# k and q over 128 partitions, transposed in two 64-row tiles; x in eight array tiles; batch 0's convolution on TensorE; PSUM and order changed

## The chip, the cores and the metric

The kernel runs on one core of one Trainium2 chip. The metric is the device time of one execution in microseconds (us). Before the change the median of three runs is 317.77 us (317.33 to 321.48).

The engines of the core run side by side, each with its own queue in order: TensorE (PE in the profile, with its weight loads as PEld), VectorE (DVE), ScalarE (ACT), GpSimd (POOL) and SyncE (SP), which here only issues DMAs. TensorE's results stand in PSUM, from where VectorE and ScalarE take them.

## The reference, cut to what matters

```python
# q, k, v: (8 batches, 8 heads, 576, 64); p: (8, 8, 32, 64); x: (8, 576, 512)
def sm_attn(qq, kk, vv):                       # softmax attention, scale 1/8
    s = scale * qq @ kk.T
    a = exp(s - max(s)); a = a / (sum(a) + 1e-9)
    return a @ vv
packed = sm_attn(p, k, v)                      # 32 rows for each head
attn   = sm_attn(q, packed, packed)            # 576 rows for each head
x      = attn with the heads side by side      # (8, 576, 512)
gate   = sigmoid(sum over kk < 5 of conv_w[kk] * x shifted down by 4 - kk rows)
out    = (gate * (x @ w_val)) @ w_out          # fp32
```

`w_val`, `conv_w` and `w_out` arrive as 64-bit floats and are turned into fp32 (or into a high and a low part) on the chip.

## The kernel before, in words

The eight heads of a batch are two groups `g` of four. In a group the four heads stand on 32 partitions each, so that scores of four heads make one tile of 128 partitions; the 576 rows of a head lie on two halves of 288 columns. A pair tile of PSUM is two banks (`big`, line 165), a single is one bank (`one`, line 168). `PSB` (line 42) sets how many of each there are: two pairs, three singles `mid`, one single `out`, eight banks in all.

The work of a batch is cut into streams, generators that yield after each step (the table `streams`, line 600). Each has a letter:

- `K`, `V`, `Q`, `P`: the loads of k, v, q and p (lines 185 to 204), all issued by SP in the written order. k and q are loaded for each group as 96 partitions x 4 heads x 3 x 128 values; a run of 128 values is two neighbouring rows of a head. For q such a run of 512 bytes stands alone in memory, for k three follow each other.
- `L`: the weights' loads (line 217); `W`, `C`, `O`: their conversion (`value_weights`, `conv_weights`, `out_weights`). `O` adds the two parts of `w_out` with two matmuls by the identity (`summed`, line 258) into a `mid` single, takes the high part off with ScalarE and the low one with VectorE.
- `k`: p is transposed (`turned`, line 324), then k (`transposed`, line 302). A k step is four transposes of 96 rows into one `mid` single, 96 columns each, then one ScalarE copy of 128x384 into `kT`. Six such steps serve a batch. `q` does the same for q.
- `a`: the packed attention (`attn_pack`, line 340): `s` matmuls in eight array tiles of 64 rows x 32 columns (`scores`, line 315) into a pair, maximum on VectorE, exponential on ScalarE, three transposes `at` of the weights by group through a `mid` single, then `pv` through a `mid` single.
- `p`, `s`, `t`: the packed result is transposed, the second attention's scores `s` are made, turned by VectorE in 32x32 blocks, normalised by VectorE, GpSimd and ScalarE, and split into a high and a low part (`attn_out`, `weighted`).
- `w`: `wp`, the packed result times `w_val` by head, into a pair (`packed_values`, line 442).
- `x` (`mixed`, line 457): attention output for the gate, by group and half: four matmuls in four array tiles of 32 rows x 64 columns, into a pair, and a ScalarE copy of 128x576 into `xp`. A batch has four such calls.
- `g` (`gate`, line 489): the convolution of the gate by channel chunk: the first tap on ScalarE, four more on VectorE (one operation of 128x576 each), tanh on ScalarE.
- `v` (`value`, line 509): twelve `val` matmuls of 288 columns into a pair, then gate times value on VectorE, the high part on ScalarE, the low part on VectorE.
- `o` (`project`, line 562): `o`, twelve matmuls of 512 columns for 128 rows of output, a copy of `osb`, a store. For the last batch the accumulators of five chunks are kept open at once in three `mid` singles, the `out` single and half a pair.

The string `ORDER` (line 46) sets the order of everything: a token such as `k3.2` runs two steps of stream `k` for batch 3. `InOrder` (line 82) ties each engine's instructions to this order, SP's DMAs too. Each tile's number of buffers is in `NB` (line 19). In the order before, TensorE's work opens with p's and k's transposes of batch 0, and SP issues two transfers of `w_val`, k's first group, six more transfers of `w_val` and then p.

A float32 matmul shows as two instructions in the trace, a transpose or a matmul on float32r as one.

Of the kernel before, what the change touches and what calls it, by code (L numbers as in the profile page):

```python
# [649 lines left out]
```

## Time and profile before

| | us |
|---|---|
| runs, median of three | 317.77 (317.33, 317.77, 321.48) |
| span of the profiled execution, first to last instruction | 320.0 |
| PE busy | 289.8 (91%) |
| DVE busy | 260.4 (81%) |
| ACT busy | 209.6 (66%) |
| POOL busy | 50.6 (16%) |

The result says no time of its own for the profiled execution beside its span. Busy time is the union of an engine's instructions; PE's ends are modelled and its matmuls overlap, so a busy PE is not PE at its peak. A row of a timeline or of the chain gives start, length, engine, operation, output tile <- input tiles and count. A row of groups gives output <- inputs, partitions x elements, the count, then busy time, mean ns of one, and the idle time of the engine ahead of them with what ended it. All lines of the kernel's own operations stand as L90, the helper `InOrder`, so groups are told by their tiles. TensorE's granted clock is 0.998 of full over the span.

### The profile page before, as it was taken

How to read it: one execution, taken by the hardware profiler on the slowest of the kernel's cores; microseconds unless marked ns; L12 is line 12 of the kernel's file. 1: busy time of each engine (PE TensorE's matmuls, PEld its weight loads, DVE VectorE, ACT ScalarE, POOL GpSimd, SP SyncE). 2: the span in 40 equal slices, each digit the busy share in tenths (PEclk: the TensorE clock that was granted, in tenths of full speed). 3: DMA queues.
4: the chain of work that ended last, by engine and by line, in shares of the span. 5: the costliest groups of instructions: out<-in, count | busy, mean ns of one | idle time of the engine just before them, and what ended most of it. 6: DMA issues, size and time to landing. Idle time of an engine off the chain costs nothing.

```text
span 320.0 us, 7365 instructions
## 1 busy us (share of the span) xinstructions
PE 289.8 (91%) x3012; PEld 211.5 (66%) x3012; DVE 260.4 (81%) x404; ACT 209.6 (66%) x424; POOL 50.6 (16%) x59
## 2 busy tenths in 40 slices
PE   0099977998989999999999999999999999999992
PEld 0067434656748876777876867877677788767881
DVE  0773599989998999899989988996899978868761
ACT  2155267988885678677967794887578755556431
POOL 1330122002300041221002312310023000230000
PEclk9999999999999999999999999999999999999999
DMA  7999999599992176941980697262402012111005
GB/s 170 218 223 268 272 231 226 111 229 172 212 221 87 37 175 136 233 126 66 215 191 35 168 209 170 62 160 81 130 33 68 35 33 69 66 66 35 33 2 165
DMA packets 42476, 43.50 MB, mean 136 GB/s; under 512 B 6085, under 2 KB 36805, under 8 KB 42442
## 3 DMA queue, kind: packets, MB, share of 16 engines
q1 hardware_dynamic: 42442, 43.02, 57.3%
q8 instruction: 24, 0.39, 0.6%
q14 instruction: 10, 0.08, 0.1%
HBM read 33.57 MB, written 9.44 MB: 134 GB/s over the span
## 4 chain that ended last, share of the span: by engine, by line
PE 84%; ACT 5%; DVE 4%; DMA 4%; issue 1%; POOL 1%; SPq 0%; ACTq 0%
PE o L90 32%; PE val L90 15%; PE s L90 6%; PE kpt L90 6%; PE qpt L90 5%; PE x L90 5%; PE pv L90 4%; PE at L90 4%; DMA p<-in_p_dram 2%; PE wp L90 2%; PE wo_sum L90 2%; DMA km<-in_k_dram 2%; ACT sig L90 1%; PE ppTt L90 1%; PE pTt L90 1%; DVE wo_words L90 1%
## 5 line engine op out<-in xcount | busy, mean ns | idle before, releaser
L90 DVE SCALAR_TENSOR_TENSOR sig<-xp,cw,sig 128x576 f32<-128x576 f32 x128 | 108.3, 846 | 7.9 <-ACT sig L90 6.7
L90 PE MATMUL o<-woh,gvh 128*128 128x512 f32 x144 | 58.8, 408 | 0.1
L90 PE MATMUL o<-woh,gvl 128*128 128x512 f32 x144 | 56.5, 393 | 0.0
L90 PE MATMUL o<-wol,gvh 128*128 128x512 f32 x144 | 56.4, 391 | 0.0
L90 PE MATMUL val<-a2h,wph 128*128 128x288 f32 x128 | 39.7, 310 | 0.0
L90 PE MATMUL val<-a2h,wpl 128*128 128x288 f32 x128 | 37.9, 296 | 0.0
L90 PE MATMUL val<-a2l,wph 128*128 128x288 f32 x128 | 37.7, 295 | 0.0
L90 POOL TENSOR_TENSOR t<-t,mx 128x576 f32<-128x576 f32 x16 | 22.5, 1404 | 90.6 <-DVE mx L90 89.1
L90 ACT COPY osb<-o 128x512 f32<-128x512 f32 x34 | 19.8, 581 | 24.3 <-PE o L90 19.3
L90 ACT ACTIVATE sig<-sig 128x576 f32<-128x576 f32 x32 | 22.0, 686 | 20.1 <-DVE sig L90 20.0
L90 PEld LDWEIGHTS o<-woh,gvh 128*128 128x128 f32 x144 | 27.0, 188 | 9.0 <-issue 2.2
L90 DVE SCALAR_TENSOR_TENSOR sig<-sig,val 128x576 f32<-128x576 f32 x32 | 23.8, 743 | 11.2 <-ACT sig L90 6.4
L90 PEld LDWEIGHTS o<-woh,gvl 128*128 128x128 f32 x144 | 27.1, 188 | 6.9 <-DVE gvl L90 0.8
L90 PEld LDWEIGHTS o<-wol,gvh 128*128 128x128 f32 x144 | 27.1, 188 | 4.5
L90 ACT CAST gvh<-sig 128x576 fp32r<-128x576 f32 x32 | 21.6, 676 | 11.3 <-DVE sig L90 10.4
L90 POOL TENSOR_TENSOR t<-t,rs 128x576 f32<-128x576 f32 x16 | 20.6, 1288 | 50.1 <-DVE rs L90 42.8
L90 DVE TENSOR_TENSOR gvl<-sig,gvh 128x576 fp32r<-128x576 f32 x32 | 25.3, 792 | 1.6 <-ACT gvh L90 1.4
L90 PE MATMUL qpt<-ident,qm 96*128 96x96 f32 x192 | 25.7, 259 | 0.9 <-DVE sm L90 0.9
L90 PEld LDWEIGHTS qpt<-ident,qm 96*128 96x128 f32 x192 | 19.6, 146 | 9.9 <-issue 5.0
L90 PE MATMUL kpt<-ident,km 96*128 96x96 f32 x192 | 25.9, 267 | 0.0
L90 PEld LDWEIGHTS val<-a2h,wph 128*128 128x128 f32 x128 | 24.1, 189 | 2.5 <-issue 1.8
L90 PEld LDWEIGHTS kpt<-ident,km 96*128 96x128 f32 x192 | 20.1, 151 | 8.3 <-issue 4.2
(78 smaller groups left out, 509.8 us busy)
## 6 DMA issues: line engine op xcount, KB each, us to landing
km<-in_k_dram SPq DMA_DIRECT2D x16, 576.0 KB, 7.3
vm<-in_v_dram SPq DMA_DIRECT2D x16, 576.0 KB, 8.3
qm<-in_q_dram SPq DMA_DIRECT2D x16, 576.0 KB, 7.4
out_dram<-osb SPq DMA_DIRECT2D x24, 256.0 KB, 2.0
wv_words<-in_moe_w_val_dram SPq DMA_DIRECT2D x8, 256.0 KB, 8.0
wo_words<-in_moe_w_out_dram SPq DMA_DIRECT2D x4, 512.0 KB, 11.6
out_dram<-osb SPq DMA_DIRECT2D x8, 192.0 KB, 3.0
p<-in_p_dram SPq DMA_DIRECT2D x16, 64.0 KB, 8.3
```

Source lines behind the costliest of these rows:

```text
L90: made = getattr(self.engine, op)(*args, **kw)
```

## The change

It alters the layout of k and q, TensorE's tiles, PSUM, where some operations run, and the order:

- k and q are loaded as 128 partitions x 9 x 128 values: partition (head, i) holds 18 neighbouring rows, one run of 4,608 bytes. v stays as it was.
- A k or q step has six transposes of 64 rows, 64 columns each, alternating between the upper and the lower half of the array's rows; the two halves write to the two banks of a pair. The ScalarE copy still has 128x384 elements, reads elements 64 apart, and writes them where `kT` or `qT` wants them (runs of 96 for k, of 3 for q).
- PSUM has three pairs, one `mid` single and one `out` single. Transposes of k and q move from `mid` to pairs.
- `x` takes both groups in one call of a half: eight array tiles of 32 rows x 64 columns, two pairs, two copies. A batch has two calls in place of four. The channels lie in another order for it, and so `w_val`, `conv_w` and `w_out` are loaded or written in that order; `w_out` by two DMAs for each chunk.
- Batch 0's convolution runs on TensorE: the packed result times each tap (GpSimd, into `kx`) is the weight of 8 matmuls for each of five taps and each half, accumulated in PSUM; tanh on ScalarE reads them from there. `gate` does nothing for batch 0. The taps are spread over partitions by 40 small matmuls and a ScalarE copy (`cwb`).
- `out_weights` drops the two matmuls by the identity: the high part comes from the top part, and GpSimd adds the rest.
- The last batch's accumulators lie in one pair, both singles, and half of another pair.
- `ORDER` is new throughout. It begins `L0 P0 K0 k0 W0 k0.2 Q0 k0.2 K0 k0 P1 k0.2 L0 W0.2 ...`: SP issues two transfers of `w_val`, p, k's first group, q's first group.

```diff
-PSB = {'big': 2, 'mid': 3, 'out': 1}
+PSB = {'big': 3, 'mid': 1, 'out': 1}
...
-            m = st[nm, b, g] = tile_of(f"{nm}m", [TP, 4, NA, 2 * D], F32, f"{nm}m_{b}_{g}")
-            sp.dma_start(m, src[b, 4 * g : 4 * g + 4].rearrange(order, a=NA, c=2))
+            m = st[nm, b, g] = tile_of(f"{nm}m", [P, NB9, 2 * D], F32, f"{nm}m_{b}_{g}")
+            sp.dma_start(
+                m, src[b, 4 * g : 4 * g + 4].rearrange("h (i n c) d -> (h i) n (c d)", n=NB9, c=2)
+            )
...
-            yield from from_double(f"wo{c}", words, P)
-            ps, hi = summed(f"wo{c}", words), woh[:, c, :]
-            yield
-            act.mul(hi, ps, 0.5)
+            yield from from_double(f"wo{c}", words, P, 0.5)
+            top, rest = st["top", f"wo{c}"], words[:, :, 0].bitcast(F32)
+            hi, lo = woh[:, c, :], wol[:, c, :]
+            act.mul(hi, top, 0.5)
             yield
             dve.scalar_tensor_tensor(
-                wol[:, c, :], ps, 0.5, hi.bitcast(F32), op0=ALU.mult, op1=ALU.subtract
-            )
+                top, top, 0.5, hi.bitcast(F32), op0=ALU.mult, op1=ALU.subtract
+            )
+            yield
+            pool.tensor_tensor(lo, top, rest, op=ALU.add)
             yield
...
-            for a in range(NA):
-                pt = one(f"{nm}pt_{b}_{g}_{a}")[:, : 4 * TP].rearrange("x (j i) -> x j i", j=4)
-                for j in range(4):
-                    pe.transpose(pt[:, j], m[:, j, a], ident[:TP, :TP])
-                yield
-                act.copy(xT[:, :, TP * a : TP * a + TP], pt)
+            if nm == "k":
+                to = xT.rearrange("x (u j) (a i b) -> x u j i b a", u=2, a=NA, i=32)
+            else:
+                to = xT.rearrange("x (u j) (i a b) -> x u j i b a", u=2, a=NA, i=32)
+            for part in range(NA):
+                pt = big(f"{nm}pt_{b}_{g}_{part}")[:, :, : 64 * NA]
+                for n in range(NA):
+                    for u in range(2):
+                        rows = slice(64 * u, 64 * u + 64)
+                        pe.transpose(
+                            pt[:, u, 64 * n : 64 * n + 64],
+                            m[rows, part * NA + n if nm == "q" else n * NA + part, :],
+                            ident[rows, rows],
+                        )
+                yield
+                act.copy(to[:, :, :, :, :, part], pt.rearrange("x u (n j i) -> x u j i n", n=NA, j=2))
                 yield
...
+            two = [big(f"x_{b}_{half}_{n}") for n in range(2)]
+            for g in range(G):
                 for hl in range(4):
                     pe.matmul(
-                        xps[D * (hl % 2) : D * (hl % 2) + D, hl // 2, :HS],
+                        two[hl // 2][D * g : D * g + D, hl % 2, :HS],
                         pp[heads[hl], g, 0, :],
                         a2[heads[hl], g, hc],
                         start=True,
                         stop=True,
                     )
-                yield
-                act.copy(xp[:, :, half, PAD:], xps[:, :, :HS])
-                yield
+            yield
+            for n in range(2):
+                act.copy(xps[n][:, :, half, PAD:], two[n][:, :, :HS])
+                yield
+
+    def convolved(b):
...
+        for half in range(2):
+            a2 = st["a2", b]
+            two = [big(f"x_{b}_{half}_{n}") for n in range(2)]
+            for back in range(NT):
+                src = (half + back) % 2
+                skip = (back + src - half) // 2
+                for g in range(G):
+                    for hl in range(4):
+                        pe.matmul(
+                            two[hl // 2][D * g : D * g + D, hl % 2, skip:HS],
+                            kx[heads[hl], g, NT - 1 - back, :],
+                            a2[heads[hl], g, src * HS : src * HS + HS - skip],
+                            start=(back == 0),
+                            stop=(back == NT - 1),
+                        )
+            yield
+            for c in range(NC):
+                act.activation(
+                    sigs[c][:, half * HS : half * HS + HS],
+                    two[c // 2][:, c % 2, :HS],
+                    AF.Tanh,
+                    scale=0.5,
+                )
+                if c % 2:
+                    yield
...
     def gate(b):
+        if b in WHOLE:
+            return
...
-            accs = {c: one(f"o_{b}_{c}") for c in range(4, 7)}
-            accs[7] = one(f"o_{b}_7", "out")
+            ends = big(f"o_{b}_4")
+            accs = {4: ends[:, 0], 5: ends[:, 1], 6: one(f"o_{b}_6"), 7: one(f"o_{b}_7", "out")}
+            last = big(f"o_{b}_8")
```

More of the change, by code (lines that the diff above doesn't have):

```diff
@@ L178, in packed_attention_gated_conv @@
     wol = const.tile([P, NC, DM], F32R, name="wol")
+    cwb = const.tile([P, G, NT, D], F32, name="cwb")
     cw = const.tile([P, NC, NT], F32, name="cw")
@@ L256, in from_double, with paired @@
         yield
-    def summed(nm, words):
-        ps = one(f"{nm}_sum")
-        pe.matmul(ps, ident, st["top", nm], start=True, stop=False)
-        pe.matmul(ps, ident, words[:, :, 0].bitcast(F32), start=False, stop=True)
-        return ps
+    def paired(x):
+        return x.rearrange("a (j g d) -> a g j d", g=G, d=D)
     def value_weights(b):
@@ L277, in conv_weights @@
         top = st["top", "cw"]
-        dve.tensor_tensor(top, top, words[:, :, 0].bitcast(F32), op=ALU.add)
+        taps = words[:, :, 1].bitcast(F32)
+        dve.tensor_tensor(
+            paired(taps),
+            top.rearrange("a (g j d) -> a g j d", g=G, d=D),
+            words[:, :, 0].bitcast(F32).rearrange("a (g j d) -> a g j d", g=G, d=D),
+            op=ALU.add,
+        )
         yield
@@ L281, in conv_weights @@
         for c in range(NC):
-            pe.transpose(cps[:, c * 8 : c * 8 + NT], top[:, c * P : c * P + P], ident[:NT, :NT])
+            pe.transpose(cps[:, c * 8 : c * 8 + NT], taps[:, c * P : c * P + P], ident[:NT, :NT])
         yield
         dve.tensor_copy(cw, cps[:, : 8 * NC].rearrange("a (c e) -> a c e", e=8)[:, :, :NT])
+        yield
+        spread = big("spread")[:, :, : NT * D]
+        for g in range(G):
+            for kk in range(NT):
+                for j in range(4):
+                    pe.matmul(
+                        spread[heads[j], g, kk * D : kk * D + D],
+                        ident[:NT, kk : kk + 1].broadcast_to([NT, NP]),
+                        taps[:, (2 * j + g) * D : (2 * j + g) * D + D],
+                        start=True,
+                        stop=True,
+                    )
+        yield
+        act.copy(cwb.rearrange("a g k d -> a g (k d)"), spread)
         yield
@@ L474, in mixed @@
                     )
+            yield
+            for n in range(2):
+                act.copy(xps[n][:, :, half, PAD:], two[n][:, :, :HS])
                 yield
-                act.copy(xp[:, :, half, PAD:], xps[:, :, :HS])
-                yield
+    def convolved(b):
+        kx = tile_of("xp", [P, 2, 2, PAD + HS], F32, f"kx_{b}")
+        kx = kx.rearrange("a n c m -> a (n c m)")[:, : G * NT * D]
+        kx = kx.rearrange("a (g k d) -> a g k d", g=G, k=NT)
+        pool.tensor_tensor(
+            kx,
+            st["ppd", b][:, :, 0, :].unsqueeze(2).broadcast_to([P, G, NT, D]),
+            cwb,
+            op=ALU.mult,
+        )
+        yield
+        sigs = []
+        for c in range(NC):
+            st["sig", b, c] = tile_of("sig", [P, S], F32, f"sig_{b}_{c}")
+            sigs.append(st["sig", b, c])
+        for half in range(2):
+            a2 = st["a2", b]
[3 more added lines that the diff above has]
+                skip = (back + src - half) // 2
+                for g in range(G):
+                    for hl in range(4):
+                        pe.matmul(
+                            two[hl // 2][D * g : D * g + D, hl % 2, skip:HS],
[3 more added lines that the diff above has]
+                            stop=(back == NT - 1),
+                        )
+            yield
+            for c in range(NC):
+                act.activation(
[3 more added lines that the diff above has]
+                    scale=0.5,
+                )
+                if c % 2:
+                    yield
     def shifted(x, back):
@@ L572, in project @@
                 yield
-            accs[8] = big(f"o_{b}_8")[:, 0]
+            accs[8] = last[:, 0]
             for n4 in range(NC - 1):
```

99 lines of the change are left out of this document (54 added, 45 removed).

## The prediction

> **What bounds the kernel now.** I read the page first: its span, the busy shares of the engines and the chain that ended last.
>
> ```profile
> span 320.0 us, 7365 instructions
> PE 289.8 (91%) x3012; PEld 211.5 (66%) x3012; DVE 260.4 (81%) x404; ACT 209.6 (66%) x424; POOL 50.6 (16%) x59
> PE 84%; ACT 5%; DVE 4%; DMA 4%; issue 1%; POOL 1%; SPq 0%; ACTq 0%
> ```
>
> TensorE holds 84% of the chain, but VectorE is busy for 260 us and is the next limit. The span has no single owner, so I cut it into four stages with the view of stretches (columns: length, then busy time of PE, PEld, DVE, ACT, POOL; clock; DMA share; GB/s).
>
> ```profile
> 0.00:16.11 16.11, 0.00 (x1) 0.03 (x1) 6.72 (x11) 3.31 (x4) 3.58 (x10) 1.00 0.91 194
> 16.11:96.34 80.23, 72.78 (x876) 46.08 (x877) 65.35 (x110) 58.95 (x131) 13.20 (x13) 1.00 1.03 217
> 96.34:303.88 207.54, 206.69 (x2089) 157.35 (x2088) 181.48 (x277) 143.57 (x284) 33.78 (x36) 1.00 0.40 104
> 303.88:320.00 16.12, 10.31 (x49) 8.04 (x47) 6.82 (x10) 3.80 (x6) 0.00 (x0) 0.95 0.26 83
> ```
>
> Up to 16.1 us TensorE does nothing. Up to 96 us it is interrupted, with the DMA engines full (share 1.03). From there to 304 us it never stops (206.7 of 207.5), and VectorE runs beside it at 87%. The third stage shortens with TensorE's own work until VectorE is full. To see what that work costs, I took the chain of waits in a part where TensorE alone carries it (start, length, group of instructions).
>
> ```profile
> 137.85 0.65 PE s L90 x16
> 138.50 0.48 PE kpt L90 x4
> 138.97 0.33 PE qpt L90 x4
> 139.31 0.22 PE at L90 x2
> 139.53 1.02 PE wp L90 x16
> ...
> 148.36 0.65 PE x L90 x8
> 149.01 1.79 PE val L90 x12
> ...
> 151.99 0.81 PE pv L90 x48
> ...
> 153.83 1.59 PE val L90 x12
> ...
> 200.38 1.13 PE s L90 x32
> ...
> 231.85 0.65 PE s L90 x16
> 232.50 0.86 PE wp L90 x16
> ```
>
> Each group costs what its columns cost, plus about 0.15 us when the group before it used the array in another tile shape. Four 96-column transposes take 0.33 us behind a full-array group and 0.48 behind `s` or `pv`. The second of two `s` calls adds 1.13 − 0.65 = 0.48; `wp` falls from 1.02 to 0.86 behind `s`, which has its shape; `val` grows from 1.59 to 1.79. Both directions pay.
>
> From these rows I priced every TensorE step and counted the steps and the changes of shape in the written order of before: 96 groups of k and q transposes × 0.33 = 31.7; 48 `at` × 0.22 = 10.6; 32 `s` × 0.48 = 15.4; 32 `x` × 0.49 (0.65 less one change) = 15.7; 16 `pv` × 0.67 = 10.7; 8 `wp` × 0.86 = 6.9; 16 groups of two full transposes × 0.22 = 3.5; 32 `val` × 1.59 = 50.9; 432 `o` matmuls × 0.23 = 99.4, which an `o` row below gives (2.78 for 12); 16 `wo_sum` at a `wp` round each (0.86 for two rounds of 512 columns, so 0.43) = 6.9; 151 changes × 0.15 = 22.7. The sum is 274.4 us. What is left of the span, 45.6 us, is 16.1 before the first matmul, some 6 behind TensorE's work at the end (10.3 busy of the last stage's 16.1), and 23.5 of interruptions and slow start, nearly all ahead of 96 us.
>
> ```profile
> 98.09 2.78 PE o L90 x12
> ```
>
> **The change part by part, TensorE first.** A k or q step becomes six transposes of 64 columns in two tiles of 64 rows, so three rounds if the two tiles run at once. `s` shows that an upper and a lower 64-row tile do: its 16 instructions lie in eight tiles, two row tiles over each of four column tiles, and take 0.48 us, no more than the 0.49 of the 8 instructions of `x` in four tiles that share no rows or columns, with the same 288 columns each. A round of 64 columns costs 0.67/12 = 0.056 us in `pv` (48 instructions, four tiles). A 128-column load has never been seen to need more than the 0.33/4 = 0.083 of a full transpose. I take 0.057, nearest in columns; 0.083 is the dear end, and a round below 0.056 no row suggests. So 96 × (0.33 − 0.17) saves 15.3 us (7.7 at the dear end).
>
> The Trainium skill, "TensorE: Matmul & The Clock Gate", section "LDWEIGHTS (loading the stationary operand)", has a load take its columns over 1.2, whatever the rows: 107 ns for these 128. By it a round is bound by its load, a step stays at 0.32 us, 14.4 of the 15.3 are gone and the time would be 313, an estimate from that page. The trace speaks against it, with loads of 128 columns hidden inside 83 ns.
>
> `x` runs 14 calls of eight tiles in place of 32 of four. If four row tiles above one another in the same columns overlap (the trace shows two, in `s`), a call stays at 0.49, 6.9 us in all. Batch 0's convolution adds two calls of five taps, 10 × 0.49 = 4.9. Net −3.9. Were the eight tiles to run as two fours, it would be +7.9.
>
> `wo_sum` leaves TensorE: −6.9. Spreading the taps adds 40 small products in four column tiles, 20 rounds × 0.056 = +1.1. The new order, counted the same way with the transposes as a shape of their own, has 186 changes: 35 × 0.15 = +5.3.
>
> TensorE's sum: 274.4 − 15.3 − 3.9 − 6.9 + 1.1 + 5.3 = 254.7, that is −19.7.
>
> The other engines, from the groups view (busy, mean ns of one, idle before):
>
> ```profile
> L90 DVE SCALAR_TENSOR_TENSOR sig<-xp,cw,sig 128x576 f32<-128x576 f32 x128 | 108.3, 846 | 7.9 <-ACT sig L90 6.7
> L90 ACT COPY kT<-kpt 128x384 f32<-128x384 f32 x48 | 22.9, 483 | 2.2 <-PE kpt L90 2.0
> L90 ACT COPY xp<-x 128x576 f32<-128x576 f32 x32 | 20.7, 646 | 1.4 <-PE x L90 1.0
> L90 ACT ACTIVATE sig<-xp,cw 128x576 f32<-128x576 f32 x32 | 24.6, 769 | 0.1
> L90 ACT ACTIVATE sig<-sig 128x576 f32<-128x576 f32 x32 | 22.0, 686 | 20.1 <-DVE sig L90 20.0
> L90 POOL TENSOR_TENSOR wv<-wv_top,wv_words 128x512 f32<-128x512 f32 x4 | 5.3, 1336 | 16.3 <-DVE wv_words L90 16.3
> ```
>
> VectorE loses batch 0's 16 taps: 16 × 0.846 = −13.5, to 246.9. `wol` stays one operation, and its final add goes to GpSimd, 4 × 1.34, plus one product for batch 0 of like size; GpSimd is 16% busy, so this costs nothing unless VectorE waits on it. ScalarE loses four first taps, four tanh and four copies (8.4 us) and gains eight half tanh and one copy of the taps, some 4.5 by 0.85 ns for an element ((646 − 483)/192). Its copies out of the transposes keep their 384 elements but read them 64 apart, and write runs of 3 for q. No row reads so. The cheap end is the 0.48 us of now; two elements' time for one would be 0.48 + 0.33 = 0.81, or +31 us on an engine 66% busy, still under TensorE. I take the cheap end; the dear one is priced as a rival.
>
> PSUM: three pairs now serve transposes, `s`, `wp`, `x` and `val`; one single serves `at`, `pv` and the small transposes. An `at` step must therefore wait for the copy of the one before. The rows below are two such steps in a row after `x`: the columns of the first are through some 0.26 after its start, about 119.50, its copy ends at 120.07, 0.57 later, or 0.7 with the release. In the new order 14 of these hand-overs have less TensorE work between them than that, short by 4.6 us in sum; behind a waiting `at` everything on TensorE queues, `o` and `val` too. About 20 of the pairs' hand-overs are as close. I add +5, between 0 (they fall into idle time early) and +10.
>
> ```profile
> 119.24 0.64 PE L90 MATMUL at<-ident,a 128*96 128x128 f32 x4
> 119.70 0.37 ACT L90 COPY a1t<-at 96x256 f32<-96x256 f32 x1
> ```
>
> The start, from the timeline:
>
> ```profile
> 0.73 1.22 SPq L90 DMA_DIRECT2D wv_words<-in_moe_w_val_dram  x2
> ...
> 2.62 3.75 SPq L90 DMA_DIRECT2D wv_words<-in_moe_w_val_dram  x6
> 5.75 1.28 ACT L90 ACT_TABLE_LOAD   x1 [5.75 <-DMA wv_words<-in_moe_w_val_dram]
> 6.42 2.19 SPq L90 DMA_DIRECT2D p<-in_p_dram  x2
> 16.11 0.66 PE L90 MATMUL pTt<-ident,p 128*128 128x128 f32 x2 [16.11 <-DMA p<-in_p_dram]
> ```
>
> ```profile
> km<-in_k_dram SPq DMA_DIRECT2D x16, 576.0 KB, 7.3
> ```
>
> TensorE waits for p, queued behind six more weight transfers. The new order issues p right behind the first two weights and k behind that. The weights land at 5.8, p a little later, a group of k, 0.59 MB, at 217 GB/s 2.7 us on: the first transposes of k at 9 to 10 instead of 16.6. What is late next is the data behind it: the second stage moves 17.4 MB with full DMA engines, and the new order wants K, V and Q of four batches by much the same point. So this gain of 7 us shrinks: 0 if DMA holds the stage, 7 if VectorE does, which has 13.5 less to do there. q comes in runs of 4,608 bytes instead of 512, k instead of 1,536, which I cost at nothing: the DMA engines are full only there (share 1.03, then 0.40). I take −4.5.
>
> Sum: 320.0 − 19.7 + 5 − 4.5 = 300.8 of span. The runs' median is 317.77 and the page does not say which run it profiled; its span is 2.2 over the median, so I take these off: **298.5 us**, rounded.
>
> VectorE's cover: stage three sheds 54 transpose groups (8.6) and half of 24 `x` calls (5.9) and takes some 3 of changes, 207.5 to 196, against the same 181.5 of VectorE, 93% full. Stage two ran it at 65.35 of 80.23, 81%.
>
> **The rivals.** *VectorE becomes the bound.* For: 93% is more than any long stage reached, and by the counted order VectorE's work stands level with TensorE's from batch 1 to batch 6. Against: it works ahead through four `sig` buffers. At 89% that stage takes 181.5/0.89 = 204, 8 more: 306.
>
> *Tiles do not overlap.* Transposes one after another are six rounds, 0.34 a step, and cost 16.4 more: 315. `x` as two fours costs 11.8: 310. Loads of 128 columns that do not hide behind 64 streamed ones hold a round at up to 0.083, 7.5 more: 306. For the last: no row has such loads behind so few columns. Against the first two: `s`.
>
> *The start pays in full* and the hand-overs nothing: 298.5 − 2.5 − 5 = 291.
>
> *The strided copies, the slower side.* At four times the time per element a copy takes 0.48 + 0.98 and ScalarE 206 + 94 = 300 busy; with the 6 us before its first work, and the last 16 in which it did 3.8, it ends near 318, some waits added: 324. It decides from about 1.25 us a copy, where ScalarE passes TensorE's 280. For: nothing in the trace reads 64 apart. Against: `t` and `sig` operations cost the same 0.7 to 0.85 us on all patterns seen. The Trainium skill, "Advanced Engine Details and Errata", section "Memory Cachelines", warns that PSUM wants two consecutive elements and gives no price; no run here shows it yet.
>
> **How the numbers follow.** Forecast 298.5 with its own spread 292 to 303: 0.52. VectorE: 0.20. Early start: 0.10. Tiles and loads: 0.12, a third of it each. Copies: 0.06. For 8 in 10 the range runs from 286 to 312, the start and the hand-overs at their cheap ends and a little of TensorE below, the `x` case and part of the first tile case above. Two per cent, 6.4 us, is what a measurement of this kernel tells from no change: faster means under 311.4. Forecast, VectorE and early start, less 0.02 for their upper tails, and the loads' 0.04 and half of `x` give faster 0.86; the rest of the tile cases and the tails same, 0.08; the copies slower, 0.06.
>
> **What would show it.** Right: the chain's k and q steps at 0.17 us (0.32 after a change of shape), `x` of 32 instructions at 0.65, first TensorE work before 10 us, copies of `kT` near 0.48, TensorE over 97% busy from about 90 us. VectorE: gaps on TensorE released by `sig` or `sm`, VectorE over 95%. Wrong at the root: a `kpt` step at 0.34, or copies above 0.8.

## The result and the profile after

The changed kernel takes 308.61 us (median of five runs, 306.13 to 309.82), the kernel before 317.78: a ratio of 0.9675 with a 95% interval of 0.9604 to 0.9746, so it is faster. The forecast was 298.5 us. The direction was right; the gain is about half of what was forecast, and the time lies inside the stated range of 286 to 312 but outside the forecast's own spread of 292 to 303. Where one execution of a run stood more than 1.5% above its fastest, the median without it is given beside the median.

The page of after: the span, the busy time of each engine, and the engines' shares of the chain that ended last.

```profile
span 304.3 us, 8095 instructions
...
PE 278.2 (91%) x3396; PEld 202.0 (66%) x3396; DVE 249.2 (82%) x388; ACT 207.2 (68%) x421; POOL 58.0 (19%) x62
...
PE 53%; DVE 26%; ACT 10%; issue 4%; DMA 2%; POOL 2%; SPq 2%; ACTq 0%; DVEq 0%; POOLq 0%
```

The profiled execution took 306.13 us, the fastest of the five. TensorE's share of the chain fell from 84% to 53%, VectorE's rose from 4% to 26%. The stretches from TensorE's first work on, with stage two of before in three parts (length; busy time of PE, PEld, DVE, ACT, POOL; clock; DMA share; GB/s):

```profile
6.14:30.00 23.86, 16.86 (x232) 9.59 (x232) 12.34 (x26) 13.28 (x31) 3.85 (x3) 1.00 1.05 291
30.00:60.00 30.00, 27.79 (x544) 16.07 (x544) 22.84 (x41) 21.39 (x50) 10.65 (x8) 1.00 0.78 191
60.00:90.26 30.26, 26.03 (x396) 18.58 (x394) 23.47 (x42) 23.11 (x53) 7.95 (x8) 0.94 0.64 181
90.26:289.10 198.84, 197.31 (x2181) 149.68 (x2180) 184.10 (x275) 145.40 (x284) 34.83 (x36) 1.00 0.38 116
289.10:304.30 15.20, 10.25 (x49) 8.08 (x47) 6.44 (x9) 3.50 (x6) 0.00 (x0) 1.00 0.27 86
```

TensorE starts at 6.14 us in place of 16.11. Stage three (the fourth line) has TensorE busy in 99% and VectorE in 92.6%. The clock of 0.94 in the third line comes from a slow stretch right behind a stall (0.61 from 69 to 72 us), told below. The chain of waits shows the steps as forecast, and something that before did not have there: long pieces of VectorE.

```profile
94.43 0.82 DVE sig L89
95.25 0.67 DVE gvl L89
...
112.06 0.67 PE x L89 x16
...
115.25 1.60 PE val L89 x12
...
123.19 0.33 PE kpt L89 x6
123.53 0.19 PE qpt L89 x6
...
129.49 0.72 DVE sig L89
130.21 0.66 DVE mx L89
130.87 0.98 DVE sig L89
```

A tiled transpose step takes 0.19 us behind another one and 0.33 behind a group of another shape.

The stall, in the timeline between 64.9 and 70.5 us (start, length, engine, operation, in brackets the idle time before it and what ended it), from the queues of GpSimd, ScalarE and TensorE:

```profile
65.83 1.53 POOL L89 TENSOR_TENSOR t<-t,mx 128x576 f32<-128x576 f32 x1 [4.37 <-DVE mx L89]
67.33 1.27 POOL L89 TENSOR_TENSOR wol<-wo_top,wo_words 128x512 fp32r<-128x512 f32 x1
68.63 0.67 ACT L89 CAST gvh<-sig 128x576 fp32r<-128x576 f32 x1 [3.96 <-POOL wol L89]
69.81 0.61 PE L89 MATMUL val<-a2h,wph 128*128 128x288 f32 x1 [3.76 <-ACT qT L89]
```

The first `gvh` has no use for `wol`. But `gvh` lies in the pool `late`, in the memory that the pool `stage` gives up (the end of the function shows the one pool closed and the other opened), and the last reader of `stage` is GpSimd's final add into `wol`. GpSimd does that add in order, behind a softmax product that waits for VectorE's maximum. Behind `gvh` ScalarE has the copy `qT`, and for that TensorE waits.

### The profile page after: what moved, and what is told of

Same layout as the page of the kernel before. It is cut to its first block, busy times and chain, and to the rows that moved or that the text cites. A ratio compares the mean times of both kernels' runs of the same rounds, so it can differ in the third digit from the quotient of the medians.

```text
span 304.3 us, 8095 instructions
## 1 busy us (share of the span) xinstructions
PE 278.2 (91%) x3396; PEld 202.0 (66%) x3396; DVE 249.2 (82%) x388; ACT 207.2 (68%) x421; POOL 58.0 (19%) x62
## 4 chain that ended last, share of the span: by engine, by line
PE 53%; DVE 26%; ACT 10%; issue 4%; DMA 2%; POOL 2%; SPq 2%; ACTq 0%; DVEq 0%; POOLq 0%
PE o L89 20%; DVE sig L89 14%; PE val L89 12%; PE x L89 4%; PE s L89 4%; PE pv L89 3%; PE at L89 3%; DMA wv_words<-in_moe_w_val_dram 2%; DVE mx L89 2%; DVE t L89 2%; ACT sig L89 2%; PE qpt L89 2%; PE kpt L89 2%; SPq L89 2%; DVE gvl L89 2%
## 5 line engine op out<-in xcount | busy, mean ns | idle before, releaser
L89 DVE SCALAR_TENSOR_TENSOR sig<-xp,cw,sig 128x576 f32<-128x576 f32 x112 | 97.4, 870 | 6.5 <-ACT sig L89 5.0
L89 PE MATMUL o<-woh,gvh 128*128 128x512 f32 x144 | 58.9, 409 | 0.8 <-ACT osb L89 0.7
L89 PE MATMUL o<-woh,gvl 128*128 128x512 f32 x144 | 56.4, 392 | 0.0
L89 PE MATMUL o<-wol,gvh 128*128 128x512 f32 x144 | 56.3, 391 | 0.0
L89 PE MATMUL val<-a2h,wph 128*128 128x288 f32 x128 | 40.8, 319 | 4.7 <-ACT qT L89 4.5
L89 POOL TENSOR_TENSOR t<-t,mx 128x576 f32<-128x576 f32 x16 | 23.7, 1481 | 87.8 <-DVE mx L89 87.8
L89 PE MATMUL val<-a2h,wpl 128*128 128x288 f32 x128 | 38.4, 300 | 0.0
L89 PE MATMUL val<-a2l,wph 128*128 128x288 f32 x128 | 38.3, 299 | 0.0
L89 POOL TENSOR_TENSOR t<-t,rs 128x576 f32<-128x576 f32 x16 | 20.6, 1288 | 69.3 <-DVE rs L89 34.0
L89 PEld LDWEIGHTS o<-woh,gvh 128*128 128x128 f32 x144 | 27.0, 188 | 9.1 <-ACT osb L89 2.8
L89 ACT ACTIVATE sig<-sig 128x576 f32<-128x576 f32 x28 | 19.3, 688 | 18.4 <-DVE sig L89 18.2
L89 PEld LDWEIGHTS o<-woh,gvl 128*128 128x128 f32 x144 | 27.0, 188 | 6.2
L89 PEld LDWEIGHTS val<-a2h,wph 128*128 128x128 f32 x128 | 24.6, 192 | 9.4 <-ACT qT L89 4.9
L89 DVE TENSOR_TENSOR gvl<-sig,gvh 128x576 fp32r<-128x576 f32 x32 | 25.0, 783 | 6.6 <-ACT gvh L89 6.6
L89 PEld LDWEIGHTS o<-wol,gvh 128*128 128x128 f32 x144 | 27.1, 188 | 4.7
L89 ACT COPY osb<-o 128x512 f32<-128x512 f32 x34 | 20.0, 589 | 14.1 <-PE o L89 13.7
L89 ACT CAST gvh<-sig 128x576 fp32r<-128x576 f32 x32 | 21.6, 676 | 11.5 <-DVE sig L89 7.4
L89 ACT COPY qT<-qpt 128x384 f32<-128x384 f32 x48 | 26.8, 564 | 3.2 <-PE qpt L89 3.1
L89 DVE SCALAR_TENSOR_TENSOR sig<-sig,val 128x576 f32<-128x576 f32 x32 | 23.7, 742 | 5.5 <-ACT sig L89 3.0
L89 ACT COPY kT<-kpt 128x384 f32<-128x384 f32 x48 | 22.5, 482 | 5.6 <-PE kpt L89 5.1
L89 PEld LDWEIGHTS val<-a2h,wpl 128*128 128x128 f32 x128 | 24.7, 193 | 0.2
L89 PEld LDWEIGHTS val<-a2l,wph 128*128 128x128 f32 x128 | 24.7, 193 | 0.0
```

What stands on the lines that cost most here:

```text
L89: made = getattr(self.engine, op)(*args, **kw)
```

## The experiments

Each is the changed kernel with the edit shown, unless another kernel is named. Where an edit changes the file, the rows have the line L61 in place of L89. Several texts below use one mark in time: the start of batch 0's third `val` call (a batch has four calls of twelve matmuls). The expectations take it for the second batch's first. That it is batch 0's third shows in two_products, where only batch 0 keeps the product `val<-a2l,wph`: its 16 matmuls stand between 63.1 and 86.1 us, on both sides of the mark at 81.1.

My theory after the result: the largest missing piece is this wait (call it the `wol` wait), and TensorE sets stage three, as forecast. The rivals: VectorE sets stage three; the early start is worth nothing, since the weights bound the load phase; the hand-overs of the single PSUM tile cost the rest.

**wol_early, wol_early_2: the last output-weight chunk earlier in the order**

```diff
-... P3 k3 O0 q1 k3 v0 K3 ... q1 O0 s1.2 k3 w1 O0 s1 a2 O0.2 | ...
+... P3 k3 O0 q1 k3 O0.3 v0 K3 ... q1 O0 s1.2 k3 w1 s1 a2 | ...
```

> The changed kernel with one thing moved: the last chunk of the output weights (its five steps, GpSimd's last add into wol among them) stands earlier in the written order, ahead of batch 1's reciprocal and the product t that follows it on GpSimd, so that the add no longer runs behind a product that waits for VectorE's maximum. My theory (the wait of ScalarE's first gvh for this add, 3.96 us, with TensorE idle for 3.8 us and at a lower clock after it, is the largest piece missing from the forecast): 302 to 306 us, 3 to 6 below the changed kernel's 308.6, the wait gone from the profile, and the granted clock nearer 1.0 than the 0.957 to 0.986 of the unprofiled runs. The rival (VectorE, 92.6% busy in stage three, sets the time there, and the stall is filled again out of its backlog): within 1 us of 308.6, the lag of TensorE behind its counted work at 280 us still near 44.

> The kernel wol_early again beside the changed kernel on one chip. If the wait for the last add into wol costs the time: 3 to 4 us below the changed kernel of this set. If the 3.5 us seen between runs on different chips were the chips: within 1 us.

Measured: 305.07 us (304.23 to 307.02). Beside the changed kernel on one chip, 305.42 (304.61 to 306.95, ratio to before 0.9625, 0.9584 to 0.9665) against 309.88 (308.05 to 312.35, 0.9755, 0.9695 to 0.9814): 4.5 us less. The stretch from 60 us to the third `val` call, first in the changed kernel's second execution, then in wol_early_2:

```profile
60.00:81.80 21.80, 17.57 (x305) 11.95 (x303) 15.89 (x27) 15.22 (x36) 6.58 (x8) 0.84 0.49 135
```

```profile
60.00:78.80 18.80, 16.82 (x334) 10.71 (x317) 17.58 (x28) 15.45 (x37) 7.24 (x8) 1.00 0.56 153
```

VectorE does 1.7 us more in 3 us less, and the clock keeps to 1.00. The `wol` wait is shown, but it is not all gone: ScalarE's first `gvh` still waits 2.0 us for `wol` (before the move 4.0), and TensorE 0.4 us for the `qT` behind it (before 3.8). The granted clock of the runs did not come out as I wrote (0.948 to 0.999 for wol_early): it is no measure of the wait.

**after_2: the changed kernel again**

> The changed kernel again, as the measure for the other runs of this set, on the same chip: 306 to 310 us. If the early stall is the same in this execution, the second batch's first val product starts 17 to 18 us after the first batch's.

Measured: the 309.88 us above; batch 0's first to third `val` call 18.4 us (63.4 to 81.8). In the first execution it was 17.6 (60.4 to 78.0), in both of wol_early's profiled executions 14.1 (64.7 to 78.8). So the first call comes later there, and the 4.5 us of the medians are what is left of the gain behind it.

**two_products, one_tap_less, both_less: what bounds stage three**

In batches 1 to 7 two_products leaves out the `val` product with the low part of the attention weights, one_tap_less one of VectorE's four taps, both_less both; their sums are not whole.

```diff
+                        if b and x is al:          # two_products, both_less
+                            continue
...
+                if kk == 1:                        # one_tap_less, both_less
+                    yield
+                    continue
```

> The changed kernel without one of VectorE's two-operand taps of the convolution (tap 1) in batches 1 to 7: this part of the sum is left out, 28 instructions of 0.87 us, 24.4 us less work on VectorE, nothing changed on TensorE. If TensorE sets the time (the forecast), it gains only what TensorE now waits for VectorE in stage three, 0 to 4 us: 304 to 308.6 us. If VectorE, 92.6% busy there, is the bound or shares it (the rival), 6 to 12 us: 297 to 302 us.

> The changed kernel without the third of the three products of val (the one of the low part of the attention weights) in batches 1 to 7: this part of the sum is left out, 112 matmuls of 0.299 us, 33 us less work on TensorE, VectorE's work as it was. If TensorE alone sets stage three, 25 to 33 us less than the changed kernel's 308.6: 276 to 284 us. If VectorE bounds stage three nearly as tightly as TensorE (the removed tap gave 3.4 us of its 24.4, the whole transposes cost 3.1 of a counted 6), it gains no more than VectorE's idle time there, some 14 us: 294 to 303 us.

> The changed kernel with both cuts at once: the third product of val left out in batches 1 to 7 (112 matmuls; what they take from TensorE's order is their spacing of 0.139 us, some 15 us, and not the 33 us that was put on them from their durations) and tap 1 of VectorE's convolution left out there (24.4 us). Each cut alone took 1.9 and 3.4 us off the changed kernel. If VectorE and TensorE bound stage three one right behind the other, the two together take 12 to 18 us off, several times the sum: 291 to 297 us, and some 210 us from the second batch's first val product to the end in place of 226.3. If something else sets the time there (ScalarE, the chain through the few buffers), the sum of the two, 4 to 7 us: 302 to 305 us.

Measured: 305.21 (303.49 to 307.36) with a tap less, 306.73 (304.60 to 310.47; 305.87 without the slowest) with a product less, 292.19 (291.18 to 296.13; 291.32 without the slowest) with both. The expectation of two_products was mis-sized by me: it took the product's duration, 0.299 us, where matmuls overlap. A call of twelve takes 1.60 us in the chain above, so its four matmuls of that product are 0.53, and 28 calls 15 us.

The load phase differs from run to run, so I read these from batch 0's third `val` call to the end. In the changed kernel that call starts at 78.0:

```profile
L89 PE MATMUL val<-a2h,wph x1: 378/378/378, 78.0 to 78.0; 128*128 128x288 f32 x1
```

The stretches from there to the end: the changed kernel (two executions), then two_products, one_tap_less, both_less.

```profile
78.00:304.30 226.30, 219.61 (x2408) 166.45 (x2406) 201.20 (x303) 159.76 (x313) 36.55 (x38) 1.00 0.39 119
```

```profile
81.80:308.10 226.30, 219.63 (x2408) 166.47 (x2406) 201.22 (x303) 159.70 (x313) 36.58 (x38) 1.00 0.40 119
```

```profile
81.10:305.80 224.70, 210.69 (x2296) 152.13 (x2294) 201.10 (x303) 158.80 (x313) 36.63 (x38) 1.00 0.40 119
```

```profile
80.80:303.30 222.50, 217.26 (x2408) 165.83 (x2406) 179.67 (x275) 159.57 (x313) 33.91 (x38) 1.00 0.40 121
```

```profile
77.80:289.40 211.60, 205.10 (x2296) 151.66 (x2295) 180.38 (x275) 158.63 (x313) 33.96 (x38) 1.00 0.42 127
```

The stretch is 226.3 us both times, whatever the load phase did. 15 us less of TensorE's work takes 1.6 off it, 21.5 us less of VectorE's 3.8, both together 14.7. So two bounds lie one right behind the other: with VectorE relieved the rest needs 222.5, with TensorE relieved 224.7, and nothing else holds the stretch above 211.6. That the two engines' waits on each other add the last 1.6 to 3.8 us is a reading. Both "TensorE sets it" and "VectorE sets it" fall. TensorE's busy time misleads here: without 15 us of its work it still reads 210.7 of 224.7.

**full_transposes: k and q in whole transposes of 96 rows**

```diff
-            m = ... tile_of(f"{nm}m", [P, NB9, 2 * D], ...)    # 64-row tiles, 18 transposes a half
+            m = ... tile_of(f"{nm}m", [TP, 4, NA, 2 * D], ...)
+                pt = big(...)[:, 0, : 4 * TP].rearrange("x (j i) -> x j i", j=4)
+                for j in range(4):
+                    pe.transpose(pt[:, j], m[:, j, a], ident[:TP, :TP])
```

> The changed kernel with k and q loaded over 96 partitions again and transposed by 12 whole transposes of 96x128 for a half of the heads, in place of 18 rounds of two 64-row tiles; PSUM, the order, batch 0's convolution and the weights stay as changed. If TensorE sets the time, the rounds' 15.3 us of counted TensorE work come back, less 0.15 us for each of some 40 to 90 changes of tile shape that go: 318 to 324 us. If VectorE sets it (the rival), a good part of these 15 us is hidden: 309 to 315 us. If the loads matter (42,000 packets again), the start lengthens by up to another 3 us in either case.

Measured: 311.74 us (311.35 to 314.29), 3.1 over the changed kernel's first median. From the third `val` call on:

```profile
83.10:309.80 226.70, 221.57 (x2292) 173.40 (x2290) 200.80 (x300) 157.58 (x312) 36.28 (x38) 1.00 0.46 119
```

and in the chain of waits:

```profile
97.22 0.33 PE kpt L61 x4
97.56 0.33 PE qpt L61 x4
...
102.19 0.48 PE qpt L61 x4
```

Stage three pays 0.4 us. Two reasons. A whole step takes 0.33 us behind a full-array group, and so does a tiled one, which pays a change of shape there. Counted over TensorE's instructions in the trace, the whole transposes have 122 changes in place of 186: by the prediction's prices 15.3 us more in steps, 64 × 0.15 = 9.6 less in changes, 5.7 net, of which 3.6 lie behind the third `val` call. That VectorE hides most of these 3.6 is a reading; it fits two_products, where 15 us of TensorE's work were worth 1.6. The rest came in the load phase, where this kernel is back at 42,540 packets; whether the packets are the cause was not tried.

**conv_back: batch 0's convolution on VectorE again**

```diff
-WHOLE = (0,)
+WHOLE = ()
+... 24 tokens g0 between the last x0 and the first x1 ...
```

> The changed kernel with batch 0's convolution on VectorE again (its 16 two-operand taps of 0.87 us, 13.9 us of VectorE, its four first taps and the copies of x on ScalarE; TensorE loses the convolution's 160 matmuls, about 4 us net of the x product); the taps stand between batch 0's last x step and batch 1's first in the written order. If TensorE sets stage three and its start, it is no slower: 304 to 309 us. If VectorE's lateness sets the time from the first val product on, the 13.9 us go nearly whole into the stretch in which batch 0 and 1 overlap: 315 to 322 us.

Measured: 321.25 us (317.89 to 325.22; 321.10 without the slowest), 12.6 over the changed kernel, and not to be told from before (1.0048, 0.9980 to 1.0117). From the third `val` call, at 91.7 us and not 78.0, it is nearly as long as the others:

```profile
91.70:319.00 227.30, 220.58 (x2408) 167.52 (x2406) 201.30 (x300) 158.93 (x311) 36.34 (x37) 1.00 0.39 115
```

13.7 us stand ahead of that mark, 12.7 of them between batch 0's first and third `val` call: 30.3 us in place of 17.6, with 26.0 of VectorE's work in place of 12.4. So the 13.9 us of taps come back nearly in full, and of the parts that were taken back one by one the convolution pays most. That VectorE bounds this stretch fits, but is not shown alone: TensorE's longest stop there is again the wait for the `qT` behind `gvh`, 6.1 us in place of 3.8, so part of the 12.6 runs through the `wol` wait. Where I put the taps may add to it; another place was not tried.

**weights_first: the value weights' loads ahead of k**

```diff
-L0 P0 K0 k0 W0 k0.2 Q0 k0.2 K0 k0 P1 k0.2 L0 W0.2 k0.2 W0 q0 K1 k0 L0 k0 q0 W0 V0 L0 W0.2 ...
+L0.4 P0 K0 k0 W0 k0.2 Q0 k0.2 K0 k0 P1 k0.2 W0.2 k0.2 W0 q0 K1 k0 k0 q0 W0 V0 W0.2 ...
```

> The changed kernel with the loads of all four chunks of the value weights issued ahead of everything else, so that the first load of k and with it TensorE's first transposes come some 6 to 9 us later, and VectorE's conversion of the weights runs without gaps. If the early start of TensorE is worth what the forecast put on it (4.5 us, up to 7), this is 4 to 7 us slower than the changed kernel's 308.6: 313 to 316 us. If the stretch up to 60 us is bounded by the weights on their way through DMA queue, ScalarE and VectorE (my reading of the changed kernel's trace, where the 10 us earlier start had shrunk to 1.7 by 62 us), it is within 2 us: 306 to 310.5 us.

Measured: 313.81 us (312.30 to 314.50), 5.2 more (3.9 over after_2's median). The first k transposes start at 14.4 us in place of 7.5, the third `val` call at 84.1, and the rest takes 226.3 again. My reading, that the early start is lost, falls: 6.9 us of it are worth 4 to 5.

**before_again: the kernel before, profiled once more**

> The kernel before, unchanged, profiled a second time: the profiled execution on which the forecast was made lasted 321.5 us, 3.7 above its median, while that of the changed kernel was 2.5 below its own. If the 3.7 us lay in one place (the load phase or the end), the time between the second batch's first val product and the end is the same here as in that execution (241.2 us) and the rest is shorter; if all stages were a little slow, it is 238 to 239 us. Expected run: 316 to 318 us.

Measured: 317.42 us. The stretch from the third `val` call to the end, and the first 60 us:

```profile
74.10:315.30 241.20, 233.35 (x2374) 177.01 (x2371) 204.68 (x308) 162.70 (x322) 36.77 (x40) 1.00 0.43 111
```

```profile
0.00:30.00 30.00, 13.63 (x172) 9.82 (x174) 15.32 (x28) 12.83 (x29) 6.10 (x12) 1.00 1.03 217
30.00:60.00 30.00, 25.15 (x318) 14.05 (x312) 27.84 (x49) 22.16 (x49) 5.12 (x5) 1.00 1.13 242
```

241.2 us, as in the first execution (78.8 to 320.0). The execution on which the forecast was made had lost its 4.7 us in the load phase.

**less_vector: wol_early, and GpSimd takes twelve of VectorE's `gvl`**

```diff
-            dve.tensor_tensor(lo, gv, hi.bitcast(F32), op=ALU.subtract)
+            eng = pool if n4 % 2 and 0 < b < B - 1 else dve
+            eng.tensor_tensor(lo, gv, hi.bitcast(F32), op=ALU.subtract)
```

> The kernel wol_early (the last output-weight chunk ahead) with, besides, GpSimd instead of VectorE computing the low part gvl of two of the four chunks in batches 1 to 6: 12 instructions of 0.79 us, 9.5 us less on VectorE, 12 of some 1.3 us more on GpSimd, which is 19% busy. If VectorE costs stage three 3.8 us over what TensorE needs (the time from the second batch's val to the end fell from 226.3 to 222.5 us with a tap less), most of that comes back: 301 to 304 us, 224 us or less from that point. If GpSimd's late products of the softmax take its place as the wait: 304 to 308 us.

Measured: 307.15 us (305.50 to 308.41), with a ratio to before of 0.9643 where wol_early has 0.9629: no gain. From the third `val` call it takes 228.7 us in place of 226.3. Against the changed kernel VectorE lost 9.5 us of work, but only 2.7 of busy time. Its groups between 120 and 280 us, first in the changed kernel, then here:

```profile
L89 DVE SCALAR_TENSOR_TENSOR sig<-xp,cw,sig 128x576 f32<-128x576 f32 x83 | 72.7, 876 | 5.4 <-ACT sig L89 4.4
...
L89 DVE SCALAR_TENSOR_TENSOR sig<-sig,val 128x576 f32<-128x576 f32 x21 | 15.6, 741 | 2.1 <-PE val L89 1.2 <-ACT sig L89 0.8
...
L89 DVE STREAM_TRANSPOSE t<-s 128x576 f32<-128x576 f32 x10 | 7.6, 765 | 0.1
L89 DVE TENSOR_TENSOR a2l<-a,a2h 128x576 fp32r<-128x576 f32 x10 | 7.5, 752 | 0.1
```

```profile
L61 DVE SCALAR_TENSOR_TENSOR sig<-xp,cw,sig 128x576 f32<-128x576 f32 x83 | 76.0, 916 | 7.8 <-ACT sig L61 6.6
L61 DVE SCALAR_TENSOR_TENSOR sig<-sig,val 128x576 f32<-128x576 f32 x21 | 15.6, 745 | 4.2 <-PE val L61 2.6 <-ACT sig L61 1.5
L61 DVE TENSOR_TENSOR a2l<-a,a2h 128x576 fp32r<-128x576 f32 x10 | 8.5, 852 | 0.1
...
L61 DVE STREAM_TRANSPOSE t<-s 128x576 f32<-128x576 f32 x10 | 7.6, 764 | 0.1
```

Operations with two large inputs in SBUF (the on-chip memory of all tiles that are not in PSUM) got slower (876 to 916, 752 to 852 ns). Those with one did not (765, 764), nor did `sig<-sig,val`, whose second input lies in PSUM (741, 745). That is where most of the missing gain in busy time went. Why the stretch is 2.4 us longer stays open.

**two_singles: wol_early, and the other single PSUM tile for `at` and `pv` in batches 0 and 1**

```diff
-                at = one(f"at_{b}_{g}_{a}")...
+                at = one(f"at_{b}_{g}_{a}", "out" if b < 2 and a == 1 else "mid")...
-            pv = one(f"pv_{b}_{g}")
+            pv = one(f"pv_{b}_{g}", "out" if b < 2 else "mid")
```

> The kernel wol_early with the other single PSUM tile (free until the first output products, at 86 us) taking every second transpose of a1 and the pv product in batches 0 and 1, so that these do not wait for ScalarE's copy out of the one tile at each step. If the hand-overs of the one tile, 5 us by the waits of the first 30 us and 5 us in the forecast, lie on the path: 2 to 5 us below wol_early. If the first 60 us are bounded by the weights on their way through DMA queue, ScalarE and VectorE: within 1 us of it.

Measured: 303.66 us (300.92 to 307.57; 303.26 without the slowest; 0.9550 of before, 0.9495 to 0.9605), 1.8 under wol_early_2. The two intervals (0.9584 to 0.9665 for wol_early_2) overlap, so a gain is likely and its size is open. It has the lowest median of the versions that compute the whole, 6.2 us below the changed kernel on the same chip.

## Why the prediction was right in direction and too low by 10 us

**The step that failed: GpSimd's add "costs nothing unless VectorE waits on it".** VectorE does not wait on it, ScalarE does, through memory. The term was 0 and measured 4.5 us (wol_early_2). The rows of before already held the same wait, short and behind another engine, in the timeline of ScalarE:

```profile
70.86 0.67 ACT L90 CAST gvh<-sig 128x576 fp32r<-128x576 f32 x1 [0.94 <-PE wo_sum L90]
```

Before, the last readers of `stage` were the two matmuls by the identity, on TensorE; whatever comes last in `stage` holds up the first writer in `late`. The change put GpSimd's queue there.

**The second: stage three "shortens with TensorE's own work until VectorE is full", with VectorE at 93% taken as not full.** It was full enough. With VectorE relieved the stretch is 222.5 instead of 226.3, so some 3.8 us of the miss hang on it. VectorE's work also came to 249.2 us in place of the 246.9 of the prediction: its taps rose from 846 to 870 ns in the mean (the last section shows what lengthens single taps). The signs that the prediction set for being right came out nearly all (steps at 0.19 and 0.33 us, first TensorE work at 6.14, `kT` at 482 ns, TensorE busy in 99% from 90 us), and so could not tell: TensorE's 99% stands beside a second bound. The rival "VectorE becomes the bound" named the mechanism and had 306; it asked for VectorE over 95%, and 92.6% was already enough. It fits the profiled run (306.13) better than the forecast, but that is in part luck: the larger part of the miss, the `wol` wait, was not in its story.

**TensorE's sum, −19.7, held as work; as time it did not.** The steps came out as priced: 0.19 us behind one of their kind for 0.17, 0.33 after a change of shape for 0.32, twelve `val` in 1.60 for 1.59. Of batch 0's two convolution calls the first has 2.65 in the chain and the second 3.12 in the timeline, 5.8 us in all for 4.9:

```profile
48.58 0.33 PE kpt L89 x6
48.92 2.65 PE x L89 x80
```

```profile
53.33 3.12 PE L89 MATMUL x<-a,kx 32*64 32x288 f32 x80
```

An `x` call has 0.67 in the first chain for 0.65; "`x` of 32 instructions" was a slip, a call has 16. The term of the transposes was −15.3 with +5.3 for changes of shape set beside the whole sum; the changes belong to the transposes, which bring 64 of them. Net they are worth 5.7 of TensorE's work, and full_transposes measured 3.1 us. The Trainium skill, "TensorE: Matmul & The Clock Gate", section "LDWEIGHTS (loading the stationary operand)", would have held a step at 0.32 us even with its six loads two at a time, an estimate from its 107 ns for a load; the trace says 0.19 and differs from it.

**The convolution was priced by the wrong engine.** The prediction gave it +4.9 on TensorE and took VectorE's −13.5 as cover. conv_back shows the reverse: 12.6 us of the time hang on those taps, nearly all ahead of the third `val` call. That VectorE's lateness there is the reason fits the rows but is not shown alone, since part goes through the `wol` wait.

**The start.** −4.5 was about right by itself: a delay of 6.9 us costs 4 to 5 (weights_first). **The hand-overs.** +5 was too dear, if anything: giving batches 0 and 1 a second tile is worth some 1.8 us, unresolved.

**The base.** I took 2.2 us off for the profiled execution's place above the median; its surplus was 4.7 us of load phase (before_again). From that execution: 315.3 − 19.7 is 295.6; the changed kernel's median run has a span of 306.7. Taken as if they simply added, of these 11.1 us the `wol` wait has 4.5, VectorE in stage three 3.8, the hand-overs perhaps 1.8. As the start should have brought 4 to 5 besides, some 5 to 6 us of the load phase stay without an owner. What the rows show there: by 60 us VectorE has done 35.2 us of work (12.34 + 22.84) against before's 43.2 (15.32 + 27.84). Of 249.2 and 260.3 in all, 214 and 217 remain, so VectorE has hardly less ahead of it than before. That the slower conversion of the weights is the reason is an argument and not shown.

**The copies.** `kT` stayed at 0.48 us as taken, so the slower rival is out; `qT`, with its runs of 3, went from 487 to 564 ns, 3.7 us in all that the prediction had at nothing. Whether they cost time was not tried.

```profile
L90 ACT COPY qT<-qpt 128x384 f32<-128x384 f32 x48 | 23.2, 487 | 1.9 <-PE qpt L90 1.5
```

```profile
L89 ACT COPY qT<-qpt 128x384 f32<-128x384 f32 x48 | 26.8, 564 | 3.2 <-PE qpt L89 3.1
...
L89 ACT COPY kT<-kpt 128x384 f32<-128x384 f32 x48 | 22.5, 482 | 5.6 <-PE kpt L89 5.1
```

## What to carry to other kernels

When the first engine's work is cut by more than the second engine's idle time allows, forecast the second: here, with 93% of a stage, it already shared the bound, and only taking work from both showed how near the two lie. Work handed to an idle engine is free only if nobody waits for its last write, and memory that is used again by another pool makes engines wait that share no data. A tiled step must be priced with the changes of shape that it brings: here they took 9.6 of the 15.3 us that the tiles saved.

## What the runs showed of the hardware that was not expected

GpSimd slows VectorE's operations with two inputs in SBUF: the taps by 5% and `a2l` by 13% between 120 and 280 us, where it is busy for 45 us in less_vector and for 29 in the changed kernel (the fifth busy time in these stretches), and leaves one-input operations alone.

```profile
120.00:280.00 160.00, 158.75 (x1744) 119.98 (x1743) 148.52 (x221) 116.45 (x226) 29.22 (x30) 1.00 0.37 111
```

```profile
120.00:280.00 160.00, 158.62 (x1751) 119.39 (x1744) 145.28 (x210) 115.76 (x226) 45.46 (x41) 1.00 0.37 112
```

The means hide what happens. Of the 83 taps of the changed kernel in this stretch 58 meet no GpSimd operation and take 810 ns in the mean; the 25 that meet one take 1031. In less_vector the taps that meet none take 810 ns as well. Here a tap starts 0.10 us behind a GpSimd product and ends 0.61 us behind its end:

```profile
199.17 1.16 POOL L89 TENSOR_TENSOR t<-t,rs 128x576 f32<-128x576 f32 x1 [4.73 <-DVE sm L89]
```

```profile
199.27 1.68 DVE L89 SCALAR_TENSOR_TENSOR sig<-xp,cw,sig 128x576 f32<-128x576 f32 x1
```

All eight taps of the changed kernel that take over 1.2 us started while such a product ran, and end 0.61 to 0.62 us behind it: the tap is held until the product is through. By the difference of the means this is some 25 × 0.22 = 5.5 us of VectorE's time in this stretch, an estimate.

The Trainium skill, "GPSIMD Engine Reference", section "1. Specifications", says that its memory interface is shared with VectorE for instructions with two SBUF inputs; these runs agree, and put the price on it.

TensorE's clock fell to half in parts of the load phase, in other places in each execution. The rows of the clock, in 40 slices of the span (tenths), of the changed kernel, of wol_early, and of wol_early_2, which is the same kernel:

```profile
PEclk9999999997999999999999999999999999999999
```

```profile
PEclk9986555899999999999999999999999999999999
```

```profile
PEclk9999987999999999999999999999999999999998
```

In wol_early the clock was 0.55 from 21 to 54 us, with TensorE busy for 86% of it:

```profile
21.00:54.00 33.00, 28.42 (x450) 16.27 (x458) 21.31 (x42) 19.52 (x45) 10.50 (x8) 0.55 1.03 233
```

It cost little. Both of wol_early's profiled executions reach the first `val` call at 64.7 us, at a mean clock up to there of 0.76 in one and 0.95 in the other; and wol_early's four runs have 307.02, 304.23, 304.36 and 305.78 us at mean clocks of 0.948, 0.959, 0.980 and 0.999, in no order. That TensorE waits for other engines in these stretches anyway is a reading. That the clock takes only the full or half rate, and that the point at which it first changes varies from run to run, is in the Trainium skill, "TensorE: Matmul & The Clock Gate", section "What's actually happening"; the trace agrees with both: seven windows of 3 us in a row, from 33 to 54 us, read 0.50 in wol_early, and the rows above differ from each other. The kernel before, with its later start, kept 0.985 to 0.999 in every run; why the new order meets the slow clock and that one does not stays open.
